# One chip core, attention and a Mish layer: another table for the order of the instructions, with 22 summed sets in place of 17

## The chip, the core and the metric

The kernel runs on one core of a Trainium2 chip. The metric is the device time of one execution in microseconds. The kernel before the change has a median of 687.55 us over 3 runs (686.66 to 688.27).

## The reference

An attention branch and a dense branch with Mish share one input and are mixed by a gate per row (S = 2048 rows, D = 640 columns, 32 heads of 20 columns, F = 1536):

```python
q, k, v = split((x @ wqkv), heads=32)            # Dh = 20
p = softmax(q @ k^T * Dh ** -0.5)
a = (p @ v).reshape(B, S, D) @ wo
h = x @ w1 + b1
b = (h * tanh(softplus(h))) @ w2                 # Mish
g = sigmoid((x * gate_w).sum(-1, keepdims=True))
out = g * a + (1 - g) * b
```

## The kernel before

**Tiles.** Work goes by groups: a group G is four heads (p, 8 of them) by 512 query rows (qc, 4 of them), 32 groups in all. A group's scores are 16 key tiles j by four heads, that is 64 units of 128 keys by 512 queries, each one a matmul on 32 rows of TensorE (L1120) into one of seven banks of PSUM. The eighth bank, `acc`, takes the products of the exponentials with V (L1155), four matmuls of a key tile side by side on the columns of the array.

**Two ways to an exponential.** 1380 of the 2048 units go to ScalarE, one to three banks in one instruction (L1138, the ring `E`). The other 668 go to VectorE: L618 writes an integer whose bits are a rough power of two (tile `T`), and GpSimd corrects it by adding a constant to the bits (L648, `int64_add` on four units at once, 128x2048 two-byte numbers). A set is four such units. A plain set is multiplied three times: as VectorE left it, and after two additions, each time with another scaled copy of V (`VD`, made from `VA` by VectorE at L600). A summed set has one addition, then VectorE sums the two versions (L672, 128x2048), then a second addition; it is multiplied twice. So a summed set costs one sum on VectorE, and saves four matmuls of 512 columns.

**The end of a group.** When a group's last product is in `acc`, VectorE transposes it (L1184), takes reciprocals of the sums (L1191, 128x16), and multiplies (L1198, 128x320, both operands in SBUF). Four transfers on SP's queue then store it to `o_dram`.

**The rest.** The projections, the dense layers and the output projection are "chains" of short matmuls, put between the score matmuls; VectorE takes each chain's result out of PSUM (L787 for q and k, L883 for the first dense layer, L925 for the second, L999 for the output, L841 for V). `Mish` is two long instructions on ScalarE (L904) with a table load on either side. Nearly all transfers stand on SP's queue in one order: loads of k and q tiles (L807, L815), stores (L790, L1231, L932), weights (L476), the second branch's rows (`bl`, L966).

**What sets the order.** A table of steps, `ORDER`, written out as text and read from left to right. Each engine gets its instructions in that order, and waits only for the data and buffers it needs:

```python
steps = {"q": load_q, "k": load_k, "b": load_b, "v": make_vd,
         "d": d_take, "D": d_unit, "S": emit_s, "x": emit_exp,
         "m": lambda: mish(act_q.popleft()), "V": emit_pv,
         "C": begin, "F": run_piece, "f": run_part, "y": vector,
         "p": lambda k, tag: waiting["G"].pop(k)[0](tag)}
for op, a in re.findall(r"([a-zA-Z])([-\d,]*)", ORDER):
    steps[op](*(int(v) for v in a.split(",") if v))
```

`S2,4` computes two score units into banks 4 and 5, `x2` exponentiates the next two on ScalarE, `D0,15,3,6` computes a unit for VectorE into bank 6, `y27` issues VectorE's 27th waiting operation, `p3,7` GpSimd's third addition into tile T7 (a negative number: in place), `V7,-1` the product of key tile 7 from `E`, `F` the next piece of a chain, `f` a quarter of a piece on 32 rows. A third number 1 in `d0,6,1` makes the set a summed one.

Of the kernel before, what the change touches and what calls it, by code (L numbers as in the profile page):

```python
# [19 lines left out]
S2,1 S1,0 S1,6 S1,5 S1,3 C0,4 F x2 C1,1 F0 F0 C3,2 x1 C4,0 F0 F0 y1 x1 F1 F C2,6 x1 x1 y3 F3 y4 F S1,1 S1,0  # L20
C6,3 S1,5 F F y6 v0,0 C5,6 y5 x1 F6 F6 F6 F6 F6 F6 F6 F6 x1 C7,0 y2 F6 F6 F6 x1 F6 F6 F5 F6 S2,1 S1,4 F5 F6 x2
F6 F6 F6 y9 y10 F5 y11 F5 y12 F5 F S2,1 S1,5 y13 y14 S1,3 x1 F C8,4 F7 F7 F7 x2 F V1,-1 x1 V0,-1 F F S2,1 x1
S2,5 F F x2 y15 C9,3 V3,-1 F F F8 F F8 x2 S3,0 F x3 F F8 S2,5 V2,-1 F8 F8 F8 F8 F8 y16 F8 F8 C10,3 F8 d0,6,1
x2 F8 F8 F8 F8 S2,0 F y17 y18 y19 C11,5 x2 F10 y20 F10 S1,2 S1,6 y21 x1 l3 S1,4 F F F10 V5,-1 F10 d0,8,0 F F
S2,1 x1 V4,-1 x1 q1 F F F F y22 F F F D0,15,3,6 S2,3 y23 V6,-1 F F x2 S1,0 S1,2 C12,1 F F11 F11 F11 F11 F11 x2
F11 F11 y24 y25 x1 S1,6 D0,15,2,3 x1 y26 x1 S1,4 F F y27 y28 y29 S1,2 D0,15,0,5 S1,0 x1 F C13,3 F12 y30 F x1 F
S1,6 S1,4 D0,14,3,2 d1,0,0 x1 S1,5 F F F x1 y31 x2 C14,0 F F y32 F D0,15,1,6 S1,1 y33 S1,2 F y34 V7,-1 F F F F
S2,3 D0,14,0,5 F F F F y35 x2 F F S1,6 S1,1 D0,14,1,2 d1,2,0 V9,-1 F V8,-1 F x2 F F F p1,3 F S1,3 y36 S2,4 x1
C15,2 F y38 F y39 V10,-1 y40 F F y41 y42 F d3,4,0 F x1 D0,14,2,6 S2,0 F F y37 y43 p3,7 F x3 V11,-1 p4,1 F S1,5
x2 y44 S1,4 y8 V15,0 y45 V14,0 x1 x1 V12,-1 S1,3 C16,4 D1,15,1,6 x1 D1,15,0,5 S1,2 y7 S2,0 y46 F F F F F p2,-1  # L30
F F x1 S1,3 D1,15,2,6 S1,2 y47 d2,3,0 F x1 V14,1 x1 F F C17,5 V15,1 y48 x1 y49 S2,0 f17,1 y50 D1,14,0,6 x1
V14,2 F D1,15,3,2 S1,3 y51 x2 S1,4 f17,2 F V13,-1 f17,0 D1,14,1,6 S1,0 q2 y52 S1,1 F x2 F p5,7 y53 x2 f17,3
D1,14,2,4 y54 y56 d1,6,0 S2,2 V0,-1 V1,-1 y57 D1,13,0,6 S2,0 p6,5 C18,5 F F d1,1,0 x2 y55 S2,2 y58 S1,4 x2 F F
F V15,0 D1,13,1,6 S1,0 y60 y61 S1,1 V15,1 V15,2 x3 D1,12,0,5 S3,2 V2,-1 x2 l8 C19,6 y62 F F F F F F F
D1,14,3,5 S2,0 V4,-1 F x3 F F y63 x2 y64 p7,8 p8,5 S3,2 V5,-1 x1 y65 V3,-1 C21,2 V14,0 D1,13,3,6 S1,0 e0 S1,1
x2 y66 D2,15,0,5 F l7 y67 F F F D1,13,2,6 S2,3 l0 V14,2 F x2 S1,0 y68 y69 D1,12,3,5 S1,1 d2,7,0 x2 y70 l2
V6,-1 x2 V13,0 D1,12,2,6 S1,2 p9,5 S2,3 d2,0,0 V14,1 x1 V7,-1 y72 V13,1 D1,12,1,5 l6 p10,8 S1,0 C20,2 S1,1 y73
V8,-1 p11,2 F F F F F F x2 p12,5 S3,3 D2,15,3,6 V12,0 y59 F F x2 V13,2 y74 F F x3 y75 S1,0 D2,15,1,6 S1,1
V12,1 V9,-1 y76 S1,3 C22,2 D2,14,0,5 S1,4 F x2 y77 x2 F F F F S2,0 D2,15,2,6 q3 F x2 l5 F F F F S1,4 y78 y79
p13,6 D2,14,3,3 v1,0 S1,5 V10,-1 C23,6 y80 V12,2 x2 y81 F D2,14,1,2 S2,0 x2 V11,-1 F F F y82 S2,3 D2,13,0,5 F  # L40
p14,8 y85 x2 F F S2,1 y86 D2,14,2,0 F F F y87 y89 V0,-1 S1,3 y90 S1,4 y91 D2,13,3,5 p15,5 V15,2 x2 V15,0 S2,0
D2,13,1,2 V15,1 y92 x2 V14,0 V1,-1 y93 d2,3,1 S1,3 x2 D2,12,0,5 S1,4 C24,2 V14,1 F e2 S2,0 x2 D2,13,2,6 y94 x2
F F D2,12,3,3 y95 y96 S2,4 d2,5,0 F F S1,0 D2,12,1,6 S1,1 y97 d3,1,0 V3,-1 x2 x2 p16,8 V14,2 V2,-1 S1,2 C25,5
y98 D2,11,0,4 y88 S1,3 V13,0 x2 F S1,0 D2,12,2,6 p17,6 S1,1 p18,2 y99 F F y101 S1,2 x2 S1,3 D2,11,3,4 F F
p19,0 S1,0 D2,11,1,6 y102 S1,1 d3,7,0 V13,1 x2 V5,-1 x2 l1 V4,-1 y103 S1,2 D3,15,0,4 y105 C26,5 S1,3 y106 F F
S1,0 x2 S1,1 D2,11,2,6 V13,2 F x2 y104 D3,15,3,4 p20,-1 S2,2 F F V12,0 S2,0 y107 V7,-1 V6,-1 x2 p21,2 S1,2
y109 D3,14,0,6 y108 S1,3 D3,14,3,5 V11,0 V12,1 D3,15,1,4 y110 y111 C27,5 x2 x2 S2,0 V11,1 V8,-1 S2,2 D3,13,0,6
y112 F F d3,2,0 y100 y113 x2 x2 F F F D3,15,2,4 S2,0 F y114 F F F D3,13,3,6 S1,2 q4 y115 S1,3 V9,-1 p22,8 x2 F
V11,2 C29,6 S2,0 D3,14,1,4 x2 V10,-1 y116 y117 y118 d3,5,0 F S1,2 k1 D3,12,0,5 S1,3 F F x2 p23,0 p24,3 x2 F
S2,0 x2 D3,14,2,4 y119 V15,0 F y120 y121 D3,12,3,5 S2,2 V15,1 V0,-1 S2,0 D3,13,1,4 y123 x2 y124 V14,0 y125  # L50
V15,2 p25,6 D3,11,0,6 d3,3,0 y126 p26,-1 S2,2 V14,1 V1,-1 C28,6 x2 D3,12,1,4 S2,0 D3,13,2,5 V2,-1 F F V14,2 F
F F x2 F y128 S2,2 x2 D3,11,3,5 S2,0 y127 x2 y129 F F F F V13,0 V3,-1 y130 S2,2 y131 y83 D3,10,0,5 S1,4 C30,6
F F y132 F x2 y84 x1 F F S1,5 y133 p27,6 S1,1 D3,10,3,0 x2 y134 x1 S1,2 V4,-1 V13,1 S1,3 D3,12,2,6 y135 C34,5
# [1392 lines left out]
```

## Time and profile before

| | |
|---|---|
| median of 3 runs | 687.55 us |
| profiled execution | 687.91 us |
| its span, first to last instruction | 686.1 us |
| granted TensorE clock | 0.999 |
| POOL (GpSimd) busy | 358.2 us, 52% of the span |
| idle time before the L648 additions | 313.4 us |
| DMA engines' busy share over the span, queue q1 | 27.1% |

In the rows of the profile each group of instructions is told by line, engine, operation, what it writes and reads, shapes and count; behind the bar stands the idle time of the engine before such instructions and who ended it. In the timeline a row gives the start in us, the length in us, and in brackets the idle time ahead of it. Neighbours of one kind are merged into one row with a count. ScalarE's first exponential starts at 9.05 us; the output's last steps on TensorE begin after 677 us.

### The profile page before, as it was taken

How to read it: one execution, taken by the hardware profiler on the slowest of the kernel's cores; microseconds unless marked ns; L12 is line 12 of the kernel's file. 1: busy time of each engine (PE TensorE's matmuls, PEld its weight loads, DVE VectorE, ACT ScalarE, POOL GpSimd, SP SyncE). 2: the span in 40 equal slices, each digit the busy share in tenths (PEclk: the TensorE clock that was granted, in tenths of full speed). 3: DMA queues.
4: the chain of work that ended last, by engine and by line, in shares of the span. 5: the costliest groups of instructions: out<-in, count | busy, mean ns of one | idle time of the engine just before them, and what ended most of it. 6: DMA issues, size and time to landing. Idle time of an engine off the chain costs nothing. (4 is left out here: it accounts for less than half of the span.)

```text
span 686.1 us, 24551 instructions
## 1 busy us (share of the span) xinstructions
PE 674.1 (98%) x10335; PEld 236.1 (34%) x10335; DVE 607.6 (89%) x1038; ACT 668.4 (97%) x705; POOL 358.2 (52%) x349
## 2 busy tenths in 40 slices
PE   8999999999999999999999999999999999999997
PEld 4433233323323343333333223222243333333333
DVE  5689999998989989999889988999998988899895
ACT  6999999999999999999999999999999999999995
POOL 5045545545454536575645544456646564565542
PEclk9999999999999999999999999999999999999999
DMA  8524331313312122121122213322321213142321
GB/s 169 119 85 79 71 76 47 72 38 79 76 31 52 41 34 39 17 48 29 53 90 48 34 52 73 66 60 34 57 64 62 22 24 67 29 69 57 51 84 59
DMA packets 128542, 40.47 MB, mean 59 GB/s; under 512 B 94960, under 2 KB 127872, under 8 KB 128432
## 3 DMA queue, kind: packets, MB, share of 16 engines
q1 hardware_dynamic: 126032, 38.29, 27.1%
q8 instruction: 81, 1.33, 0.9%
q10 hardware_dynamic: 2400, 0.62, 0.4%
q14 instruction: 29, 0.24, 0.2%
HBM read 22.29 MB, written 12.78 MB: 51 GB/s over the span
## 5 line engine op out<-in xcount | busy, mean ns | idle before, releaser
L1138 ACT ACTIVATE E<-Sp 128x1024 bf16<-128x1024 f32 (+2 forms) x687 | 636.5, 1088 | 6.1 <-PE Sp L1120 5.6
L648 POOL INT64_ADD T<-T x334 | 348.3, 1053 | 313.4 <-DVE T L618 187.8
L618 DVE TENSOR_SCALAR T<-Sp 128x512 int16<-128x512 f32 x668 | 437.8, 682 | 44.6 <-PE Sp L1120 37.3
L1120 PE MATMUL Sp<-qT,kT 32*128 32x512 bf16 x2048 | 262.7, 383 | 4.8 <-DVE T L618 2.1
L1120 PEld LDWEIGHTS <-kT 32*128 32x128 bf16 x2048 | 70.5, 91 | 237.5 <-issue 232.0
L1155 PE MATMUL Sp<-E,VA 128*21 128x512 bf16 x1380 | 128.8, 382 | 0.1
L1155 PE MATMUL Sp<-T,VD 128*21 128x512 bf16 x1268 | 117.2, 382 | 0.0
L702 PE MATMUL Sp<-w_sb,big 128*32 128x320 bf16 x1488 | 75.6, 301 | 0.0
L702 PE MATMUL Sp<-xT,w1t 128*32 128x512 bf16 x940 | 74.2, 382 | 0.0
L1155 PEld LDWEIGHTS <-VA 128*21 128x21 bf16 x2048 | 45.0, 90 | 62.8 <-issue 54.4
L1155 PE MATMUL Sp<-T,VA 128*21 128x512 bf16 x668 | 63.8, 382 | 0.0
L702 PE MATMUL Sp<-xT,ws 128*32 128x512 bf16 x716 | 55.5, 382 | 0.4 <-issue 0.3
L702 PEld LDWEIGHTS <-big 128*32 128x32 bf16 x1488 | 33.3, 95 | 28.3 <-issue 20.1
L1155 PEld LDWEIGHTS <-VD 128*21 128x21 bf16 x1268 | 29.8, 90 | 37.5 <-issue 31.8
L883 DVE TENSOR_SCALAR big<-Sp,b1f 128x512 bf16<-128x512 f32 x48 | 35.7, 743 | 3.0 <-PE Sp L702 2.2
L702 PE MATMUL Sp<-wv,xT 128*32 128x81 bf16 (+2 forms) x960 | 35.0, 256 | 0.0
L702 PE MATMUL Sp<-wo_sb,od 128*32 128x320 bf16 (+1 forms) x604 | 28.9, 300 | 0.6 <-DVE ot L999 0.6
L702 PEld LDWEIGHTS <-w1t 128*32 128x32 bf16 x940 | 20.5, 94 | 25.4 <-issue 18.8
L787 DVE CAST st<-Sp 128x512 bf16<-128x512 f32 x36 | 24.4, 683 | 4.6 <-PE Sp L702 4.4
L702 PEld LDWEIGHTS <-xT 128*32 128x32 bf16 x960 | 21.0, 96 | 11.5 <-issue 6.0
L1184 DVE STREAM_TRANSPOSE T<-Sp 128x512 f32<-128x512 f32 x32 | 22.7, 709 | 2.2 <-PE Sp L1155 1.9
L702 PEld LDWEIGHTS <-ws 128*32 128x32 bf16 x716 | 16.4, 95 | 19.3 <-issue 13.4
(84 smaller groups left out, 242.8 us busy)
## 6 DMA issues: line engine op xcount, KB each, us to landing
w1t<-in_B_w_dram SPq DMA_DIRECT2D x24, 320.0 KB
q_dram<-st SPq DMA_DIRECT2D x20, 128.0 KB
b_dram<-bt SPq DMA_DIRECT2D x16, 160.0 KB
bl<-b_dram SPq DMA_DIRECT2D x16, 160.0 KB
qT<-q_dram SPq DMA_DIRECT2D x124, 20.0 KB
o_dram<-T SPq DMA_DIRECT2D x120, 20.0 KB
out_dram<-ot SPq DMA_DIRECT2D x15, 160.0 KB
kT<-k_dram SPq DMA_DIRECT2D x28, 80.0 KB
```

What stands on the lines that cost most here:

```text
L618: nc.vector.tensor_scalar(out=dst.bitcast(I16), in0=src, scalar1=inv_sqrt_dh * LOG2E * 128.0, scalar2=127.0 * 128.0 + (BETA2 if two else B ...
L648: nc.gpsimd.int64_add(dst[:, :].bitcast(I64), src[:, :].bitcast(I64), n * 0x0001000100010001)
L702: nc.tensor.matmul(out_[k : k + 32], lhsT=lhsT[:, k : k + 32], rhs=rhs, tile_position=(0, k), start=start, stop=ch.done(), skip_group_chec ...
L787: nc.vector.tensor_copy(out=res["st"][:, :], in_=ps[:, :])
L883: nc.vector.tensor_scalar(out=big[:, pair_of(c, ft), (ft % 2) * QC : (ft % 2 + 1) * QC], in0=ps[:, :], scalar1=b1f[:, ft : ft + 1], scalar ...
L1120: nc.tensor.matmul(ps_cols, lhsT=kT[p][32 * t_ : 32 * t_ + 32, j * P : (j + 1) * P], rhs=qT[G][32 * t_ : 32 * t_ + 32, :], tile_position=( ...
L1138: nc.scalar.activation(E[:, x : x + n, :], allb[:, k0 : k0 + n, :], ACT.Exp, scale=inv_sqrt_dh,)
L1155: nc.tensor.matmul(acc[32 * t_ : 32 * t_ + DH + 1, :], lhsT=lhsT, rhs=rhs, start=(pv_done[G] == 0), stop=(pv_done[G] == pv_total[G] - 1), ...
L1184: nc.vector.transpose(out=st["T1"][:, :, :].rearrange("p b r -> p (b r)"), in_=acc[:, :])
```

## The change

Nothing but the table `ORDER` is replaced; every function stays as it is. The new text has one line more, so each line number of the kernel is one higher afterwards (L1138 becomes L1139). Its first and last steps:

```diff
 ORDER = """
-S2,1 S1,0 S1,6 S1,5 S1,3 C0,4 F x2 C1,1 F0 F0 C3,2 x1 C4,0 F0 F0 y1 x1 F1 F C2,6 x1 x1 y3 F3 y4 F S1,1 S1,0
+S1,1 S3,4 x1 C0,3 S1,0 S1,2 x2 F F x1 x1 C1,1 C2,6 F0 C3,4 F0 F0 C4,5 x1 F1 F F3 F2 y3 S1,0 C6,2 y4 S1,1 F F F
...
+V11,0 V9,-1 C183,1 V8,-1 F181 y1007 V11,1 V12,2 V10,-1 V11,2 C182,5 F F y1008 F183 F183 b15 y1009 F183 F183 F
+y1010 F y1013 y1011 y1012
 """
```

Counted over the two tables:

| | before | after |
|---|---|---|
| ScalarE exponentials of 1, 2, 3 banks | 57, 567, 63 (687) | 44, 572, 64 (680) |
| summed sets among the 167 | 17 | 22 |
| products of a key tile with V (four matmuls each) | 829 | 824 |
| GpSimd additions | 334 | 334 |
| VectorE operations that the table issues | 1008 | 1013 |
| quarter pieces `f` of chains on 32 rows | 76 | 68 |
| visits of TensorE to matmuls on 32 rows | 640 | 643 |

**VectorE at the fourth group's end (about 133 us).** `VD` is the scaled copy of V, `T_0_88` the group's output, `rec` the reciprocals. Before:

```order
L787 CAST st<-Sp 128x512
L618 TENSOR_SCALAR T<-Sp 128x512 x2
L1191 RECIPROCAL rec<-T_2708 128x16
L618 TENSOR_SCALAR T<-Sp 128x512
L600 TENSOR_SCALAR VD<-VA 128x7x84 x2
L618 TENSOR_SCALAR T<-Sp 128x512 x2
```

Now:

```order
L788 CAST st<-Sp 128x512
L619 TENSOR_SCALAR T<-Sp 128x512 x3
L601 TENSOR_SCALAR VD<-VA 128x7x84
L1192 RECIPROCAL rec<-T_2672 128x16
L601 TENSOR_SCALAR VD<-VA 128x7x84
L619 TENSOR_SCALAR T<-Sp 128x512
```

The first copy now stands directly behind the L619 that completes a set for GpSimd, and the second behind the reciprocal.

**VectorE near the end of the program (about 642 us).** Before:

```order
L618 TENSOR_SCALAR T<-Sp 128x512 x3
L1191 RECIPROCAL rec<-T_12798 128x16
L1198 TENSOR_TENSOR T_1_89<-T_12798,rec 128x16x20
L618 TENSOR_SCALAR T<-Sp 128x512
L999 SCALAR_TENSOR_TENSOR ot<-Sp,g_t,bl 128x320
```

Now:

```order
L1192 RECIPROCAL rec<-T_12781 128x16
L619 TENSOR_SCALAR T<-Sp 128x512 x3
L1000 SCALAR_TENSOR_TENSOR ot<-Sp,g_t,bl 128x320
L619 TENSOR_SCALAR T<-Sp 128x512
L1199 TENSOR_TENSOR T_1_89<-T_12781,rec 128x16x20
```

The multiplication stood directly behind the reciprocal, two places behind the L618 that completes a set; five instructions now stand between the two, and the L619 that completes a set is four places ahead.

**SP's queue in the last 35 us.** `bl` are rows of the second branch, `od` the transposed attention output. Before:

```order
L932 DMA b_dram<-bt 128x640
L953 DMA_TRANSPOSE od<-o_dram 128x512
L1008 DMA out_dram<-ot 128x640
L966 DMA bl<-b_dram 128x640
L1008 DMA out_dram<-ot 128x640
L966 DMA bl<-b_dram 128x640 x4
```

Now:

```order
L967 DMA bl<-b_dram 128x640
L954 DMA_TRANSPOSE od<-o_dram 128x512
L1009 DMA out_dram<-ot 128x640
L967 DMA bl<-b_dram 128x640
L1009 DMA out_dram<-ot 128x640
L967 DMA bl<-b_dram 128x640 x2
```

One load of `bl` goes ahead of the last transposing load of `od`, and the bunch of four becomes two, with the last one behind one more store of the output.

More of the change, by code (lines that the diff above doesn't have):

```diff
@@ L25 @@
[L25 to L29, printed above, removed]
@@ new lines @@
+p170,1 D17,14,2,6 S1,2 x2 S1,3 f104,3 x2 F p171,4 y548 F F d17,3,0 y549 S1,0 d17,2,0 S1,1 y550 C105,6
+D17,13,0,4 V10,-1 F x2 D17,14,3,5 S1,2 p172,5 S1,3 y551 V11,2 F F x2 v6,0 S2,0 D17,13,1,4 F F q18 S1,2 y552
+y553 y556 S1,3 y557 D17,13,2,5 p173,8 V0,-1 v5,0 x2 V15,1 D17,12,0,4 x2 S2,0 V14,0 p174,4 V15,0 y559 y562 S2,2
+x2 x2 D17,13,3,6 V1,-1 d17,0,0 V14,2 y563 D17,11,0,4 D17,12,1,5 y560 S2,0 V2,-1 x2 V14,1 V15,2 y564 S2,2
+p175,7 D17,12,2,6 V3,-1 y565 V13,0 D17,11,1,5 S1,0 y566 y567 S1,1 V13,1 V4,-1 x2 C106,5 S1,2 D17,12,3,6 x2
@@ new lines @@
+y648 S1,2 D20,12,1,4 y649 p205,4 S1,3 x2 y650 V13,1 V13,0 V14,2 y651 D20,11,3,1 y652 S1,5 x2 S1,6 q22 x2
+d21,7,0 D20,11,0,0 V3,-1 S2,3 p206,5 y653 D20,12,2,2 d20,3,0 V2,-1 C121,1 F F x2 D20,10,0,0 S2,5 y654 V4,-1 x2
+F S2,2 D20,11,1,4 F x2 F y655 S1,5 D20,10,3,0 S1,6 p207,6 y656 x2 H y657 p208,8 V13,2 D20,11,2,4 S2,2 V12,1
+d21,6,0 y658 y659 V12,2 D21,15,0,6 S1,0 x2 S1,1 D21,15,3,5 V12,0 V6,-1 y660 d21,0,0 V11,0 C122,6 S2,3
+D20,10,1,2 F V5,-1 x2 x2 v7,0 S1,0 f122,3 p209,-1 S1,1 y661 D21,14,0,5 F y662 p210,4 F S2,2 f122,1 y664
@@ new lines @@
+d21,5,1 D20,10,2,4 y665 x2 F x2 V11,2 S1,0 D21,14,3,5 S1,1 y666 f122,0 V11,1 V7,-1 D21,15,1,2 y667 S1,3 C123,5
+x2 f122,2 S1,4 y669 V9,-1 V10,0 x2 F S2,0 D21,13,0,6 p211,2 x2 y668 f123,3 p212,-1 V8,-1 S1,2 f123,1
+D21,15,2,4 S1,3 y670 V10,1 V10,2 F d22,4,0 S1,0 x2 y671 S1,1 D21,13,3,6 f123,0 F y663 S1,2 f123,2 S1,3
+D21,14,1,4 F y672 x2 x2 y673 d22,8,0 V0,-1 y675 S1,0 D21,12,0,6 p213,2 S1,1 V15,0 V1,-1 S1,2 D21,14,2,5 S1,3
+y677 C124,6 p214,-1 y674 V15,1 x2 F F x2 D21,12,3,4 d21,1,0 y678 S2,0 F y679 S1,2 D21,13,1,5 p215,3 S1,3 x2
```

581 lines of the change are left out of this document (285 added, 296 removed).

## The prediction

> **What bounds the kernel now.** I read the busy times first, then the waits, then stretches of the span.
>
> ```profile
> span 686.1 us, 24551 instructions
> PE 674.1 (98%) x10335; PEld 236.1 (34%) x10335; DVE 607.6 (89%) x1038; ACT 668.4 (97%) x705; POOL 358.2 (52%) x349
> DVE T L618 <- PE Sp L1120: 37.3, 105, 1.3
> ACT E L1138 <- PE Sp L1120: 5.6, 14, 1.2
> 130.00:150.00 20.00, 19.16 (x267) 5.62 (x268) 19.11 (x31) 19.20 (x20) 9.27 (x9) 1.00 0.27 61
> 150.00:430.00 280.00, 278.99 (x4167) 92.37 (x4159) 252.59 (x415) 279.46 (x287) 150.22 (x143) 1.00 0.23 50
> 430.00:450.00 20.00, 19.42 (x255) 5.15 (x247) 19.27 (x32) 19.54 (x22) 10.51 (x10) 1.00 0.27 42
> ```
>
> The columns of the stretches are: length, busy us of PE, PEld, DVE, ACT and POOL, clock, DMA share, GB/s. ScalarE (ACT) and TensorE (PE) are both full: from 150 to 430 us ScalarE works 279.46 of 280 us. The order can win only what ScalarE loses, and the fourth row says that it waits 14 times for scores from L1120, 5.6 us in all (the third is VectorE's own wait for them). In two short stretches it loses 0.80 us (130 to 150) and 0.46 us (430 to 450), and just there VectorE is as full as the others: 19.11 and 19.27 of 20 us. So the question is which late VectorE work holds up the scores.
>
> **Where the waits come from.** The price list by form, with a stretch of 14 undisturbed exponentials (291 to 303 us) as its second row:
>
> ```profile
> L1138 ACT ACTIVATE E<-Sp 128x1024 bf16<-128x1024 f32 x567 | 537.8, 1084 | 4.6 <-PE Sp L1120 4.2
> L1138 ACT ACTIVATE E<-Sp 128x1024 bf16<-128x1024 f32 x14 | 13.0, 1115 | 0.0
> L1138 ACT ACTIVATE E<-Sp 128x1536 bf16<-128x1536 f32 x63 | 95.7, 1519 | 0.5 <-PE Sp L1120 0.5
> L1138 ACT ACTIVATE E<-Sp 128x512 bf16<-128x512 f32 x57 | 33.0, 649 | 1.0 <-PE Sp L1120 0.9
> L672 DVE TENSOR_TENSOR T<-T 128x2048 bf16<-128x2048 bf16 x17 | 21.4, 1258 | 0.1
> L1198 DVE TENSOR_TENSOR T<-T,rec 128x320 bf16<-128x320 f32 x31 | 18.5, 597 | 0.2
> L600 DVE TENSOR_SCALAR VD<-VA 128x588 bf16<-128x588 bf16 x16 | 9.2, 578 | 0.0
> ```
>
> Now four places in order of time, each from VectorE's late instruction to ScalarE's idle time in brackets; the row at 428.63 is the same multiplication with nothing beside it.
>
> ```profile
> 92.49 1.04 POOL L648 INT64_ADD T<-T  x1 [3.61 <-DVE rec L1191]
> 92.51 1.36 DVE L1198 TENSOR_TENSOR T<-T,rec 128x320 bf16<-128x320 f32 x1
> 94.53 0.37 PE L1120 MATMUL Sp<-qT,kT 32*128 32x512 bf16 x1 [0.47 <-DVE T L618]
> 95.59 2.49 ACT L1138 ACTIVATE E<-Sp 128x512 bf16<-128x512 f32 x4 [0.45 <-PE Sp L1120]
> ...
> 133.39 3.12 POOL L648 INT64_ADD T<-T  x3 [1.48 <-PE Sp L1155]
> 133.56 2.10 DVE L600 TENSOR_SCALAR VD<-VA 128x588 bf16<-128x588 bf16 x2
> 136.30 0.37 PE L1120 MATMUL Sp<-qT,kT 32*128 32x512 bf16 x1 [0.82 <-DVE T L618]
> 137.70 2.05 ACT L1138 ACTIVATE E<-Sp 128x1024 bf16<-128x1024 f32 x2 [0.79 <-PE Sp L1120]
> ...
> 428.63 0.48 DVE L1198 TENSOR_TENSOR T<-T,rec 128x320 bf16<-128x320 f32 x1
> ...
> 437.87 1.28 DVE L1198 TENSOR_TENSOR T<-T,rec 128x320 bf16<-128x320 f32 x1
> 440.32 1.02 ACT L1138 ACTIVATE E<-Sp 128x1024 bf16<-128x1024 f32 x1 [0.27 <-PE Sp L1120]
> 441.53 1.94 ACT L1138 ACTIVATE E<-Sp 128x1024 bf16<-128x1024 f32 x2 [0.19 <-PE Sp L1120]
> ...
> 641.94 1.36 DVE L1198 TENSOR_TENSOR T<-T,rec 128x320 bf16<-128x320 f32 x1
> 644.46 2.51 ACT L1138 ACTIVATE E<-Sp 128x1024 bf16<-128x1024 f32 x3 [0.18 <-PE Sp L1120]
> ```
>
> The chain is the same each time. A GpSimd addition runs (92.49, 1.04 us); a multiplication that needs 0.48 us starts 0.02 us later and ends at 93.87, after the addition's end at 93.53. Everything behind it on VectorE is 0.88 us late, L618 frees a bank late, TensorE's next score waits 0.47 us, and ScalarE 0.45 us. I call this a meeting. ScalarE's idle time at the four places is 0.45 + 0.79 + 0.27 + 0.19 + 0.18 = 1.88 us. An exponential after an idle time also lasts 1.08 us in place of a step of about 0.91 us ((13.0 - 1.115) / 13): five times 0.17 is 0.85. Together 2.73 us. Two transfers cost ScalarE time too:
>
> ```profile
> 426.16 0.39 PE L1120 MATMUL Sp<-qT,kT 32*128 32x512 bf16 x4 [0.61 <-DMA kT<-k_dram]
> 426.69 3.28 ACT L1138 ACTIVATE E<-Sp 128x1536 bf16<-128x1536 f32 x3 [0.46 <-PE Sp L1120]
> ...
> 665.75 6.91 SPq L966 DMA_DIRECT2D bl<-b_dram  x4
> 668.13 0.55 DVE L999 SCALAR_TENSOR_TENSOR ot<-Sp,g_t,bl 128x320 bf16<-128x320 f32 x1 [1.00 <-PE Sp L1155]
> 668.74 0.73 PE L702 MATMUL Sp<-wo_sb,od 128*32 128x320 bf16 x16 [0.62 <-DVE ot L999]
> 669.92 6.66 ACT L1138 ACTIVATE E<-Sp 128x1024 bf16<-128x1024 f32 x6 [0.56 <-PE Sp L1120]
> ```
>
> L999 at 668.13 reads `bl`. L1155, named as its releaser, writes another bank, so I take the load issued from 665.75 on as what it waited for: an inference.
>
> **The change part by part.** First, exponentials: 13 fewer of one bank, 5 more of two, 1 more of three, the same 1380 banks in 7 fewer instructions. Durations grow 0.435 us a bank (649, 1084, 1519 ns), so of a step of 0.911 us only 0.04 belongs to the instruction: 7 x 0.04 = -0.3 us. If nothing overlapped it would be 1.084 - 0.870 = 0.21 each, -1.5; if it is hidden, 0. I take -0.3, since exponentials run back to back nearly everywhere. (The Trainium skill, "ScalarE: Activation LUTs", section "What ACT_TABLE_LOAD costs", gives 186 ns fixed and about 93 ns of overlap between neighbours; 7 x 93 ns would be -0.65, an estimate from that page; the row's 0.04 decides.)
>
> Second, TensorE: five products fewer, three more visits to the 32-row matmuls, and two pieces of a chain that were four quarters on those rows become whole. The prices:
>
> ```profile
> 304.60 0.39 PE L1120 MATMUL Sp<-qT,kT 32*128 32x512 bf16 x3
> 304.93 0.40 PE L1155 MATMUL Sp<-E,VA 128*21 128x512 bf16 x4
> 305.15 0.39 PE L1155 MATMUL Sp<-T,VA 128*21 128x512 bf16 x4
> ```
>
> A product takes 0.22 us (304.93 to 305.15), a visit to the 32-row matmuls 0.33 (304.60 to 304.93). Five products save 5 x 0.22 = 1.1; three more visits cost up to 1.0, two whole pieces up to 0.4. Between -1.1 and +0.3; I take 0, because ScalarE, as full as TensorE, keeps its own pace.
>
> Third, five more sums: 5 x 1.258 = 6.3 us on VectorE. Their cover is VectorE's idle time, 686.1 - 607.6 = 78.5 us; without it, all 6.3 us count. The 17 sums of before start no idle time of ScalarE at the places above, so I take +0.5.
>
> Fourth, the meetings. In the order of before, 7 of the 31 multiplications stand directly behind the reciprocal, three of them two places behind the L618 that completes a set: these are the ones at 92, 437 and 641 us. In the new order 5 stand so, and two of them (the 1st and the 26th) two places behind a completed set; none is at the old places. At 133 us one copy of `VD` goes ahead of the addition and one can still meet it. So -2.73 for the old places, if they all go (0 if none does). For new meetings: two multiplications as above, the second copy, two more multiplications with one instruction between, and two sums side by side where GpSimd is due, six in all. An unhidden one costs 2.73 / 5 = 0.55. I count a third of them, as VectorE has 11% to spare over the span: 6 x 0.55 / 3 = +1.1 (0 to 3.3).
>
> Fifth, transfers. Of the `bl` loads one now goes ahead of the last transposing load, and the bunch of four is broken up: -0.56 - 0.17 = -0.73 (0 if L999 waited for something else). The k tile at 426 us stands behind the same weight load as before, only the second tile's four loads no longer follow it: half of 0.46 + 0.17, -0.3 (0 to -0.63).
>
> Sum: -0.3 + 0 + 0.5 - 2.73 + 1.1 - 0.73 - 0.3 = -2.46. The profiled execution took 687.91 us, 1.8 more than its span, and becomes 685.45; the median of the runs lies 0.36 below it, so 685.1. What is late next: scores in the stretches where both engines are full, with no VectorE cause, which the order cannot give back.
>
> **The rivals.** (1) The meetings only move: all six new ones reach ScalarE, 3.3 in place of 1.1. Then -0.26, 687.3, no change. For it: the number of additions is the same, and the chances to meet grew by five sums. Against: the four costly places have all been taken apart.
>
> (2) Slower: VectorE becomes the engine that frees banks late, because of the sums. With all of 6.3 us on the path the sum is -2.96 + 6.3 = +3.3, 690.9; it turns to the slower side once 4.4 us of the 6.3 show, and 690.0 is the middle of that. For it: in the stretches at 130 and 430 us VectorE has 0.9 and 0.7 us of 20 spare, less than one sum, and a sum holds GpSimd up as well:
>
> ```profile
> 234.18 1.21 DVE L672 TENSOR_TENSOR T<-T 128x2048 bf16<-128x2048 bf16 x1
> 234.36 1.93 POOL L648 INT64_ADD T<-T  x1 [2.26 <-DVE T L618]
> ```
>
> The addition that starts during the sum lasts 1.93 us in place of 1.04, so its set is complete later and its products wait. Against: over the span VectorE has 11% to spare. (The Trainium skill, "SBUF — State Buffer", section "SBUF: two separate sides", has one lock for the pair of ports that VectorE and GpSimd share, held for a whole instruction by whoever starts first. The rows at 92 and 234 us agree; by the rule the five added sums would be 5 x 1.258 = 6.3 us more in which no addition gets on, an estimate.)
>
> (3) Deeper: no new meeting and no sum costs anything, and both transfers go: -0.3 - 2.73 - 0.73 - 0.63 = -4.4, 683.2. For it: most of VectorE's work has cover. Against: six new chances to meet.
>
> **How the numbers follow.** A measurement of this kernel can tell 0.2%, that is 1.4 us, from no change. The forecast near 685.1 has 0.43, own range 683.9 to 686.2; deeper 0.12; no change 0.24; slower 0.21. Faster is 0.43 + 0.12 = 0.55. Below, the range reaches past the deeper case by 0.8, for the unlikely -1.5 of the exponentials in part: 682.4. Above, it reaches nearly to the middle of the slower case: 689.8.
>
> **What would show it.** ScalarE's idle time before L1139 falls from 6.1 us (its wait for scores from 5.6) to about 4; the L1199 mean falls from 597 ns towards 540, L601 from 578 towards 400; no PE wait above 0.4 us for the L619 bank near 95, 136 and 440 us; no wait for `ot` near 669 us. The step on sums is wrong if VectorE's wait for scores (37.3 us at L618 before) falls by the full 6 us while ScalarE idles more. The forecast is wrong if L1199 and L601 are quicker and the time is not: then the scores were late for TensorE's own sake.

## The result and the profile after

The changed kernel has a median of 685.86 us (684.88 to 686.69, 8 runs) against 687.37 us for the kernel before on the same chip: ratio 0.9974, 95% interval 0.9963 to 0.9985. A second series gave 685.16 against 686.93 us: 0.9973 (0.9963 to 0.9984). So the change takes off some 1.5 to 1.8 us, about 0.26%, 0.7 to 1.0 us less than the sum of the prediction. One execution of the run e9_sums_small below, at a granted clock of 0.863, took 716.0 us and is left out of its median.

The profiled execution took 685.10 us. The first rows are from its page, the next three from its table of waits (waiting engine, tile, line, releaser; us in total, times, longest), the last three from its groups by form.

```profile
span 683.2 us, 24486 instructions
PE 673.0 (99%) x10315; PEld 236.4 (35%) x10315; DVE 606.5 (89%) x1043; ACT 667.3 (98%) x698; POOL 359.1 (53%) x349
...
L1139 ACT ACTIVATE E<-Sp 128x1024 bf16<-128x1024 f32 (+2 forms) x680 | 635.3, 1090 | 4.3 <-PE Sp L1121 3.9
```

```profile
DVE T L619 <- PE Sp L1121: 37.8, 101, 1.3
...
ACT E L1139 <- PE Sp L1121: 3.9, 9, 1.2
...
PE Sp L1156 <- POOL T L649: 1.4, 3, 0.6
```

```profile
L673 DVE TENSOR_TENSOR T<-T 128x2048 bf16<-128x2048 bf16 x22 | 26.7, 1219 | 0.0
...
L1199 DVE TENSOR_TENSOR T<-T,rec 128x320 bf16<-128x320 f32 x31 | 17.2, 555 | 0.2
L601 DVE TENSOR_SCALAR VD<-VA 128x588 bf16<-128x588 bf16 x16 | 5.2, 324 | 0.0
```

ScalarE waits for scores 3.9 us in place of 5.6. The copies of `VD` fell from 578 to 324 ns, the multiplications at a group's end only from 597 to 555. The third row of the waits is new in the list: three times TensorE waits for a tile of GpSimd's, 1.4 us in all; the kernel before has no such wait.

The two short stretches that were not full before are full now (length; busy us of PE, PEld, DVE, ACT, POOL):

```profile
130.00:150.00 20.00, 20.00 (x278) 5.88 (x278) 18.92 (x33) 20.00 (x21) 9.88 (x10) 1.00 0.23 52
...
430.00:450.00 20.00, 19.99 (x265) 5.68 (x261) 18.79 (x32) 20.00 (x23) 10.93 (x11) 1.00 0.34 77
```

Both tables exponentiate the same 1380 banks, so ScalarE's progress can be compared bank by bank. This table is worked out from the two traces: the start of the exponential that takes up the given number of banks done, and how far the new order is ahead. An exponential after an idle time takes some 0.17 us more than the step between undisturbed ones, so a difference can be complete a bank or two later.

```
banks done   before      after     after is ahead by
   58         37.90      37.37       0.53
   99         56.76      56.57       0.18
  181         95.59      95.05       0.54
  190         99.97      99.14       0.83
  270        137.70     135.95       1.75
  511        261.48     260.34       1.13
  851        417.51     416.07       1.44
  870        426.69     424.69       2.00
  901        441.53     438.93       2.61
  984        479.85     476.97       2.89
 1213        597.84     595.52       2.31
 1271        624.51     622.50       2.01
 1280        628.65     627.17       1.47
 1314        644.46     642.51       1.94
 1366        669.92     667.08       2.84
```

It gains at the old meetings (95 to 100, 137, 440, 480, 644 us) and at the `bl` wait (670). It loses some 0.55 us at 57 (it is 0.72 ahead at 94 banks done and 0.18 at 99), and about 0.55 to 0.8 us each near 261, 597 and 628 us. Much of the gain near 427 us belongs to this one execution of the kernel before: the runs below that keep its table are ahead by as much there.

The 0.53 us at 38 us hides two things. The three runs below that keep the table of before up to there are 0.5 to 0.7 us ahead of this execution already at 36.5 us, where the changed kernel is only 0.1 ahead; so the steps of its start cost it 0.4 to 0.5 us, by a cause that stays open. Right behind, at 37 to 40 us, it gains 0.6 us, because a meeting that the prediction had not listed is gone. In the kernel before, both copies of `VD` run beside additions:

```profile
35.48 1.09 DVE L600 TENSOR_SCALAR VD<-VA 128x588 bf16<-128x588 bf16 x1
...
36.80 0.81 DVE L600 TENSOR_SCALAR VD<-VA 128x588 bf16<-128x588 bf16 x1
...
37.40 1.57 ACT L1138 ACTIVATE E<-Sp 128x512 bf16<-128x512 f32 x3 [0.27 <-PE Sp L1120]
```

In the changed kernel they last 0.33 and 0.32 us (33.27 and 34.11 us), and ScalarE has no idle time there.

One of the three losing places, from the timeline of the changed kernel; the first fence is GpSimd alone in a narrow window, the second all engines:

```profile
591.77 1.93 POOL L649 INT64_ADD T<-T  x1 [1.47 <-DVE T L619]
```

```profile
591.59 1.22 DVE L673 TENSOR_TENSOR T<-T 128x2048 bf16<-128x2048 bf16 x1
...
594.77 0.40 PE L1156 MATMUL Sp<-T,VD 128*21 128x512 bf16 x4 [0.59 <-POOL T L649]
595.10 0.40 PE L1121 MATMUL Sp<-qT,kT 32*128 32x512 bf16 x4
...
595.52 0.60 ACT L1139 ACTIVATE E<-Sp 128x512 bf16<-128x512 f32 x1 [0.44 <-PE Sp L1121]
```

A sum starts at 591.59, an addition 0.18 us later. The addition lasts 1.93 us in place of 1.04, and the next one in GpSimd's queue is 0.89 us late. The product that reads the tile of that next one stands ahead of the next scores on TensorE and waits 0.59 us, so the scores are late and ScalarE idles 0.44 us. This is the meeting of the prediction with the roles exchanged: GpSimd is held up, and TensorE waits for it.

### The profile page after: what moved, and what is told of

Same layout as the page of the kernel before. It is cut to its first block, busy times and chain, and to the rows that moved or that the text cites. A ratio compares the mean times of both kernels' runs of the same rounds, so it can differ in the third digit from the quotient of the medians.

```text
span 683.2 us, 24486 instructions
## 1 busy us (share of the span) xinstructions
PE 673.0 (99%) x10315; PEld 236.4 (35%) x10315; DVE 606.5 (89%) x1043; ACT 667.3 (98%) x698; POOL 359.1 (53%) x349
## 5 line engine op out<-in xcount | busy, mean ns | idle before, releaser
L1139 ACT ACTIVATE E<-Sp 128x1024 bf16<-128x1024 f32 (+2 forms) x680 | 635.3, 1090 | 4.3 <-PE Sp L1121 3.9
L619 DVE TENSOR_SCALAR T<-Sp 128x512 int16<-128x512 f32 x668 | 437.8, 683 | 47.1 <-PE Sp L1121 37.8
L1156 PE MATMUL Sp<-T,VD 128*21 128x512 bf16 x1248 | 114.7, 382 | 1.4 <-POOL T L649 1.4
L703 PE MATMUL Sp<-wv,xT 128*32 128x81 bf16 (+2 forms) x960 | 37.5, 257 | 0.1
L884 DVE TENSOR_SCALAR big<-Sp,b1f 128x512 bf16<-128x512 f32 x48 | 35.7, 744 | 2.0 <-PE Sp L703 0.7
L673 DVE TENSOR_TENSOR T<-T 128x2048 bf16<-128x2048 bf16 x22 | 26.7, 1219 | 0.0
```

Source lines behind the costliest of these rows:

```text
L619: nc.vector.tensor_scalar(out=dst.bitcast(I16), in0=src, scalar1=inv_sqrt_dh * LOG2E * 128.0, scalar2=127.0 * 128.0 + (BETA2 if two else B ...
L673: nc.vector.tensor_tensor(out=d[0][:, :], in0=d[0][:, :], in1=d["T"][:, :], op=ALU.add)
L703: nc.tensor.matmul(out_[k : k + 32], lhsT=lhsT[:, k : k + 32], rhs=rhs, tile_position=(0, k), start=start, stop=ch.done(), skip_group_chec ...
L884: nc.vector.tensor_scalar(out=big[:, pair_of(c, ft), (ft % 2) * QC : (ft % 2 + 1) * QC], in0=ps[:, :], scalar1=b1f[:, ft : ft + 1], scalar ...
L1139: nc.scalar.activation(E[:, x : x + n, :], allb[:, k0 : k0 + n, :], ACT.Exp, scale=inv_sqrt_dh,)
L1156: nc.tensor.matmul(acc[32 * t_ : 32 * t_ + DH + 1, :], lhsT=lhsT, rhs=rhs, start=(pv_done[G] == 0), stop=(pv_done[G] == pv_total[G] - 1), ...
```

## The experiments

Every run was compared with the kernel before on its own chip. In the diffs only the steps around an edit are shown of each long line. The first two undo two causes in the table of before, one at a time, and the third both.

**Meetings alone.**

```diff
-q5 y136 l4 V13,2 S2,3 y137
+q5 l4 V13,2 S2,3 y137
...
-x2 y138 S1,5
+x2 y138 y136 S1,5
...
-D6,14,0,5 y142 y143 S1,2
+D6,14,0,5 S1,2
...
-S2,0 y202 V13,2
+S2,0 y202 y142 y143 V13,2
```

y646, y707 and y953 move in the same way, behind y649, y708 and y955.

> The table of before, with only five VectorE places changed: four multiplications L1198 (those at 92, 437, 476 and 641 us) and the pair of VD copies L600 (133 us) are issued a few VectorE instructions later, so that none starts right beside a GpSimd addition. Theory (meetings cost ScalarE time and TensorE can use it): the idle times 0.45 + 0.79 + 0.27 + 0.19 + 0.18 us go, with up to 5 x 0.17 us of slower first exponentials: 1.9 to 2.7 us less than before, ratio 0.9960 to 0.9973; mean of L1198 from 597 to about 510 ns, of L600 from 578 to about 390 ns. Rival (TensorE and ScalarE are both full, so a stall that is taken away comes back within a few us): VectorE's instructions get as short, but the time stays within 0.5 us of before, ratio 0.9993 to 1.0007, and ScalarE's idle time before L1138 stays near 6.1 us.

Measured: 684.39 us (684.01 to 684.65) against 687.04, ratio 0.9960 (0.9947 to 0.9972), 2.65 us less. By form:

```profile
L1138 ACT ACTIVATE E<-Sp 128x1024 bf16<-128x1024 f32 x567 | 537.8, 1087 | 2.9 <-PE Sp L1120 2.7
...
L1198 DVE TENSOR_TENSOR T<-T,rec 128x320 bf16<-128x320 f32 x31 | 15.9, 512 | 0.1
L600 DVE TENSOR_SCALAR VD<-VA 128x588 bf16<-128x588 bf16 x16 | 7.6, 483 | 0.0
```

The idle time went and did not come back, so the rival falls. The mean of `VD` fell only to 483 ns, not to 390: the moved pair lasts 0.33 and 0.32 us, but four other copies that this edit leaves, at 35, 36, 244 and 407 us, still last 0.81 to 1.09. Behind the two at 35 and 36 us ScalarE still idles 0.27 us, as in the kernel before. With the transfers untouched, this run has no wait near 426 us, but it has the one for `bl`:

```profile
664.05 0.55 DVE L999 SCALAR_TENSOR_TENSOR ot<-Sp,g_t,bl 128x320 bf16<-128x320 f32 x1 [0.93 <-DMA bl<-b_dram]
...
664.66 0.73 PE L702 MATMUL Sp<-wo_sb,od 128*32 128x320 bf16 x16 [0.54 <-DVE ot L999]
...
665.84 3.06 ACT L1138 ACTIVATE E<-Sp 128x1024 bf16<-128x1024 f32 x3 [0.49 <-PE Sp L1120]
```

Here the profile itself names the load as L999's releaser, which the prediction had inferred.

**Transfers alone.**

```diff
-S1,0 k6 S1,1 F F S1,3 y622
+S1,0 S1,1 F F S1,3 y622
...
-S1,0 y629 S1,1
+S1,0 y629 k6 S1,1
...
-V2,-1 y983 D31,13,1,0
+V2,-1 y983 b11 D31,13,1,0
...
-C176,0 b11 F x2
+C176,0 F x2
```

> The table of before, with only two transfers moved: one bl load goes ahead of where it stood (from 665.75 us to about 662 us), and the four loads of the second k tile go about 5 us later. Theory (both waits were the transfers' own): PE's wait for ot near 668.7 us (0.62) and ScalarE's idle 0.56 us behind it go, 0.7 us; at 426 us up to 0.6 us: together 0.7 to 1.3 us less, ratio 0.9981 to 0.9990. Rival (L999 waited for something else, and the k tile is late because of the weight load ahead of it): no change at both places, ratio 0.9995 to 1.0005, and the waits at 426 and 668 us stay.

Measured: 686.43 us (686.03 to 687.50) against 687.04, ratio 0.9991 (0.9982 to 0.9999), 0.6 us less. L999 no longer waits for a load, and ScalarE runs through:

```profile
665.70 3.39 ACT L1138 ACTIVATE E<-Sp 128x1024 bf16<-128x1024 f32 x4
...
666.11 0.55 DVE L999 SCALAR_TENSOR_TENSOR ot<-Sp,g_t,bl 128x320 bf16<-128x320 f32 x1 [0.17 <-PE Sp L702]
```

The wait at 426 us is absent too, but it was absent in the run ahead of it as well, which left both transfers in place. SP's queue before that time, in the kernel before, and then with the meetings moved:

```profile
419.32 1.58 SPq L476 DMA_DIRECT2D w1t<-in_B_w_dram  x1
420.95 4.34 SPq L807 DMA_DIRECT2D kT<-k_dram  x8
```

```profile
417.17 0.42 SPq L476 DMA_DIRECT2D w1t<-in_B_w_dram  x1
417.63 5.44 SPq L807 DMA_DIRECT2D kT<-k_dram  x8
```

In this run the weight load takes 1.54 us and only four loads follow it. The wait was there only where the weight load held the queue for 1.58 us and all eight loads followed it. How often that happens is not settled; the 0.6 us of this run, just under the expected 0.7 to 1.3, are no more than the `bl` wait alone is worth.

**Both.** The edits of the two runs together.

> The table of before with the edits of the two runs ahead of it together (five VectorE places and two transfers). Theory (independent stalls add up): 2.6 to 4.0 us less than before, ratio 0.9942 to 0.9962, so more than the whole change brought (1.5 us). Rival (the stalls hide one another, or the engines take them back): no more than the better of the two alone, at most 1.5 us, ratio 0.9978 or above.

Measured: 683.68 us (683.37 to 684.16), ratio 0.9951 (0.9937 to 0.9964), 3.36 us less; 2.65 + 0.61 is 3.26. The two add up, and together they bring about twice what the whole change did. So the change gave something back.

**The products that wait.** In the table of after, three steps `V` go later on TensorE, nothing else:

```diff
-V13,1 V14,0 V14,1 y383 x2 S1,0 y385 x2 S1,1 D11,12,2,6 C78,5 F x2 F V1,-1
+V13,1 V14,0 y383 x2 S1,0 y385 x2 S1,1 D11,12,2,6 C78,5 F x2 F V14,1 V1,-1
...
-V9,-1 V12,1 S1,2 C156,6 S1,3 D28,13,0,5 S1,4 F y889 F F F d28,7,0 F V10,-1
+V9,-1 S1,2 C156,6 S1,3 D28,13,0,5 S1,4 F y889 F F F d28,7,0 F V12,1 V10,-1
...
-V13,2 F x2 S1,3 D29,10,2,5 y939 S1,4 V3,-1
+F x2 S1,3 D29,10,2,5 y939 S1,4 V13,2 V3,-1
```

> The table of after, with three products of a set moved 7 to 13 steps later on TensorE. They are those at 259.52, 594.77 and 626.16 us, which wait 0.40, 0.59 and 0.39 us for a GpSimd addition that was held up behind a sum (L673). Theory (this is where the change gave time back): ScalarE's idle 0.51 + 0.44 + 0.47 us goes, 1.4 us, with 3 x 0.17 us up to 1.9 us less than after: 684.0 to 684.5 us, ratio to before 0.9946 to 0.9954. Rival (the late addition holds VectorE or the tile ring up in the same way, so the wait moves to another buffer): the time of after, 685.9 us, ratio 0.9970 to 0.9978.

Measured: 683.65 us (683.37 to 684.20), ratio 0.9950 (0.9938 to 0.9963). Bank by bank against the changed kernel, this execution gains 0.66 us at 260, 0.49 at 595 and 0.58 at 627 us, and nothing elsewhere: 1.7 us. The place shown above in this run:

```profile
591.89 5.37 ACT L1139 ACTIVATE E<-Sp 128x1536 bf16<-128x1536 f32 x6
...
593.48 0.40 PE L1121 MATMUL Sp<-qT,kT 32*128 32x512 bf16 x4
...
594.56 0.40 PE L1156 MATMUL Sp<-T,VD 128*21 128x512 bf16 x4
```

The scores now go ahead of the product, which waits for nothing, and ScalarE has no idle time.

**The new meetings.** On top of these three edits, four multiplications go clear of the additions beside them:

```diff
-S1,5 y73 p10,2
+S1,5 p10,2
...
-F y77 F F F
+F y77 y73 F F F
```

y140, y164 and y276 move behind y143, y183 and y281.

> The table of after with the three late products (as in the run e4_late_products) and four multiplications L1199 (54.1, 96.2, 121.7 and 187.4 us) a few VectorE instructions later, clear of the additions beside them. Theory (each new meeting costs only where ScalarE was seen to idle behind it: 0.25 us at 56.6, 0.17 at 123.9, each with 0.17 us of a slower first exponential): 0.4 to 0.9 us less than with the late products alone (683.65 us): 682.8 to 683.3, ratio to before 0.9937 to 0.9945. Rival (all four are covered by other work, the idle there has another cause): as with the late products alone, 683.5 to 683.8, ratio 0.995.

Measured: 683.47 us (683.26 to 685.25), ratio 0.9953 (0.9941 to 0.9964): no gain that can be told from the run with late products. L1199 fell from 555 to 488 ns. ScalarE's idle time at 56.6 us is gone, the one at 123.8 is not, though the multiplication at 121.7 was the nearest late work:

```profile
121.64 2.03 ACT L1139 ACTIVATE E<-Sp 128x1024 bf16<-128x1024 f32 x2
123.83 3.98 ACT L1139 ACTIVATE E<-Sp 128x1024 bf16<-128x1024 f32 x4 [0.17 <-PE Sp L1121]
```

Bank by bank against the run with late products, this run gains 0.48 us at 57 and loses 0.18, 0.21 and 0.15 us near 101, 126 and 194 us, behind the three places to which the other multiplications went. At 126 us, for example, L1199 and the L884 behind it now stand ahead of four L619, which start at 124.49 in place of 124.33 us, and ScalarE idles a new 0.10 us. So one of the four meetings had a price, and the other three moves cost about as much as that one brought. That those three were covered where they stood is read from the traces: behind them the changed kernel has no idle time of ScalarE but the 0.17 us at 124 us, and the kernel before has the same one (124.87 us). The expectation of 0.4 to 0.9 us was too high, and it had put that idle time down to the wrong neighbour.

**What a sum costs.** Four runs. In the first, each sum is preceded by an instruction of the same size that changes nothing:

```diff
         def total():
+            nc.vector.tensor_tensor(out=d[0][:, :], in0=d[0][:, :], in1=d[0][:, :], op=ALU.max)
             nc.vector.tensor_tensor(out=d[0][:, :], in0=d[0][:, :], in1=d["T"][:, :], op=ALU.add)
```

> The table of after, but ahead of each of the 22 sums VectorE takes the maximum of the one operand with itself, 128x2048, which changes nothing in the result: 22 more instructions of about 1.2 us, 26.5 us more of VectorE in all. The prediction's step (most of a sum is covered, 0.1 us of each shows): +2 us, 688 us, ratio to before 1.000. First rival (VectorE frees the banks late, so a sum counts in full): +20 to +27 us, 706 to 713, ratio 1.027 to 1.037. Second rival (a sum costs through the addition that it holds up: the three places where that already happens grow by 1.2 us each, and some more places begin): +4 to +8 us, 690 to 694, ratio 1.004 to 1.010.

Measured: 715.12 us (712.35 to 718.81), ratio 1.0409 (1.0386 to 1.0432). Against the changed kernel's 0.9973 that is 30 us for 22 instructions; the first rival's 27 is the nearest. TensorE's wait for banks that L619 frees grows from 0.4 to 9.2 us, and new is a wait of 7.4 us for the sums themselves; so with this much more work VectorE does free the banks late. The granted clock lay between 0.988 and 0.998 in these executions (712.35 us at 0.998, 718.81 at 0.988), so some 3 of the 30 us may be the clock's. Is a sum that dear, then? The opposite edit says no:

```diff
-            nc.vector.tensor_tensor(out=d[0][:, :], in0=d[0][:, :], in1=d["T"][:, :], op=ALU.add)
+            nc.vector.tensor_tensor(out=d[0][:, 0:16], in0=d[0][:, 0:16], in1=d["T"][:, 0:16], op=ALU.add)
```

> The table of after; each of the 22 sums adds only the first 16 of its 2048 columns, so nearly all of the summing is left out (the products and additions stay). VectorE loses about 22 x 1.1 = 24 us of work, and no addition is held up by a sum. The prediction's step (0.1 us of a sum shows) with the three held additions found since (1.4 to 1.9 us): 3.6 to 4.1 us less than after, about 681.5, ratio to before 0.991 to 0.9925. First rival (a sum counts in full, as the doubled sums did at 1.3 us each): 24 to 29 us less, 656 to 661, ratio 0.957 to 0.963. Second rival (sums are covered altogether and the held additions have another cause): 0 to 1 us less, ratio 0.996 to 0.998.

Measured: 683.42 us (683.29 to 683.87, four executions), ratio 0.9948 (0.9934 to 0.9962). VectorE has 23.3 us less to do in the 22 sums (26.7 to 3.4), and the time falls by 1.7 us (0.9973 to 0.9948). Bank by bank the gain is 0.7 us at 260, 0.6 to 0.8 from 595 to 597 and 0.4 at 627, the same three places as with the late products. That is the 1.4 to 1.9 us of the held additions alone; the further 0.1 us for each sum does not show, and the first rival, a sum that counts in full, falls for the sums that are there. The rows at the middle one:

```profile
590.96 0.16 DVE L673 TENSOR_TENSOR T<-T 128x16 bf16<-128x16 bf16 x1
591.14 2.05 POOL L649 INT64_ADD T<-T  x2 [1.47 <-DVE T L673]
...
593.24 0.40 PE L1156 MATMUL Sp<-T,VD 128*21 128x512 bf16 x4
```

Two additions take 2.05 us, none is held up, and the product comes without a wait. The third run puts only a 128x512 instruction ahead of each sum:

```diff
+            nc.vector.tensor_tensor(out=d[0][:, 0:QC], in0=d[0][:, 0:QC], in1=d[0][:, 0:QC], op=ALU.max)
```

> The table of after; ahead of each of the 22 sums VectorE takes the maximum of a 128x512 part with itself, which changes nothing in the result: about 0.3 us more each, 22 x 0.3 = 6.8 us in all. If VectorE's delay counts from the first tenth of a microsecond on, as 1.3 us for 1.2 at the doubled sums could be read: +6 to +8 us, 692 to 694, ratio to before 1.006 to 1.009. If there is cover for about one sum at each place, which the sum itself does not use up: 0 to +1.5 us, 685.5 to 687, ratio 0.997 to 0.9995. Between the two, +2 to +5, would say that some places have cover and some have none.

Measured: 693.74 us (693.29 to 694.33), ratio 1.0098 (1.0082 to 1.0113), 8.6 us above the changed kernel by the two ratios, a little more than the first expectation; the second, cover for about one more sum at each place, falls. The groups by form, and then the timeline of the place known from above (the added line makes each later line number one higher):

```profile
L674 DVE TENSOR_TENSOR T<-T 128x2048 bf16<-128x2048 bf16 x22 | 29.8, 1355 | 0.8
...
L673 DVE TENSOR_TENSOR T<-T 128x512 bf16<-128x512 bf16 x22 | 9.2, 420 | 0.1
```

```profile
599.16 0.42 DVE L673 TENSOR_TENSOR T<-T 128x512 bf16<-128x512 bf16 x1
599.34 1.13 POOL L649 INT64_ADD T<-T  x1 [1.47 <-DVE T L619]
...
599.61 1.94 DVE L674 TENSOR_TENSOR T<-T 128x2048 bf16<-128x2048 bf16 x1
...
601.60 0.40 PE L1157 MATMUL Sp<-T,VA 128*21 128x512 bf16 x4 [0.85 <-DVE T L674]
...
602.74 1.02 ACT L1140 ACTIVATE E<-Sp 128x1024 bf16<-128x1024 f32 x1 [1.01 <-PE Sp L1122]
```

The instruction lasts 0.42 us, not the 0.3 that I had expected. At this place it also turns round who starts first: the addition gets in between, and now the sum lasts 1.94 us in place of 1.22. VectorE has 9.2 + 3.1 = 12.3 us more to do, and the time grows by some 8.6. ScalarE's wait for scores shows that the price comes from many places, more of them the longer the delay: 3.9 us in 9 waits in the changed kernel, 7.3 in 15 here, 23.4 in 30 with the sums twice.

The fourth run joins the small sums and the late products:

> The table of after with both edits that each brought about 1.8 us: the sums add only 16 of their 2048 columns (most of the summing is left out), and the three late products stand later. Theory (sums cost only through the three held additions, so the two edits remove the same idle time): no less than either alone, 683.3 to 683.8 us, ratio to before 0.9945 to 0.9953. Rival (two separate causes): both gains, 3.5 us less than after, about 681.8 us, ratio 0.9922 to 0.9930.

Measured: 683.31 us (683.17 to 684.39), ratio 0.9949 (0.9937 to 0.9962), the same as either alone. The changed kernel itself once more, beside it on the same chip:

> The changed kernel itself once more, beside the run e11_small_late on the same chip. Theory (the late products and the small sums remove what the change gave back): 685.0 to 685.9 us, ratio to before 0.9970 to 0.9980, so 1.5 to 2.0 us above e11_small_late. Rival (the gains of those runs were the chip's): equal to e11_small_late within 0.5 us. The profile should show the idle times of about 0.5 us near 260, 595 and 627 us again.

Measured: 685.16 us (685.04 to 685.38), ratio 0.9973 (0.9963 to 0.9984), with idle times of 0.52, 0.45 and 0.47 us at 260.43, 595.64 and 627.28 us. So the 22 sums cost 1.8 us in all, through the additions that they hold up at three places; the bank-by-bank comparison shows nothing beyond that.

**Are these the five added sums?** Only one of them is. Followed step by step through the two tables, the sum at 591.59 us (group 27, key tile 12) is one of the five that the kernel before lacks. The sums at 256.35 us (group 11, key tile 14) and 623.88 us (group 29, key tile 12) stand in both. The first of these holds up the same addition in the kernel before, where it costs nothing. Both kernels, before and then after; the rows of GpSimd are from narrow windows:

```profile
258.30 1.20 DVE L672 TENSOR_TENSOR T<-T 128x2048 bf16<-128x2048 bf16 x1
258.47 1.93 POOL L648 INT64_ADD T<-T  x1 [1.79 <-DVE T L618]
...
261.63 0.39 PE L1155 MATMUL Sp<-T,VD 128*21 128x512 bf16 x4
```

```profile
256.35 1.20 DVE L673 TENSOR_TENSOR T<-T 128x2048 bf16<-128x2048 bf16 x1
256.52 1.93 POOL L649 INT64_ADD T<-T  x1 [1.60 <-DVE T L619]
...
259.52 0.40 PE L1156 MATMUL Sp<-T,VD 128*21 128x512 bf16 x4 [0.40 <-POOL T L649]
```

In both, the next addition ends 2.95 us after the held one starts. The product that reads its tile starts 3.16 us after that start in the kernel before; now TensorE is ready for it after 2.60 us. The new order has put it 0.56 us nearer. At 627 us the two instructions have changed places. In the kernel before, the addition (625.31 us, 1.04) stands ahead of the sum (625.90, 1.52); now it starts 0.23 us behind the sum:

```profile
623.88 1.33 DVE L673 TENSOR_TENSOR T<-T 128x2048 bf16<-128x2048 bf16 x1
...
626.16 0.40 PE L1156 MATMUL Sp<-T,VD 128*21 128x512 bf16 x4 [0.39 <-POOL T L649]
```

So of the 1.8 us some 0.6 belong to an added sum and 1.2 to the order around two sums that were there already. The kernel before has three additions held up behind a sum (1.86 to 1.93 us, at 234, 258 and 270 us) and no wait of TensorE for them; that its 17 sums cost nothing is read from this, no run tests it.

**The price of an exponential.** In the table of after, 50 steps `x2` in a row (290 to about 342 us) become `x1 x1`.

> The table of after with 50 exponentials of two banks (from 290 to about 350 us) written as two of one bank each: the same banks, 50 instructions more. The prediction's step (0.04 us an instruction, from the step between exponentials): +2.0 us, or +2.5 by two steps of 0.477 against one of 0.903; 687.9 to 688.4, ratio to before 1.0007 to 1.0015. Rival (no overlap between neighbours; 0.21 us an instruction, from the durations): +10.7 us, 696.6, ratio 1.013. In a sentence by itself: by the Trainium skill, ScalarE: Activation LUTs, section What ACT_TABLE_LOAD costs, 93 ns each would be +4.7 us, an estimate from that page.

Measured: 689.16 us (688.46 to 690.58), ratio 1.0031 (1.0019 to 1.0043), 4.0 us more by the ratios, between the step's 2.0 to 2.5 and the rival's 10.7. Bank by bank, ScalarE goes from 0.17 us ahead of the changed kernel at 289 us to 2.67 behind it at 342: 2.8 us for 50 instructions, 0.056 each. Another 0.8 us, of which some 0.3 come back soon after, is lost at one place behind the stretch:

```profile
361.42 0.40 PE L1156 MATMUL Sp<-E,VA 128*21 128x512 bf16 x4 [0.46 <-ACT E L1139]
...
361.92 1.02 ACT L1139 ACTIVATE E<-Sp 128x1024 bf16<-128x1024 f32 x1 [0.55 <-PE Sp L1156]
```

TensorE waits for an exponential that has become late, and ScalarE then for TensorE. The Trainium skill (ScalarE: Activation LUTs, What ACT_TABLE_LOAD costs) gives 186 ns fixed and about 93 ns of overlap between neighbours; 50 times the 93 ns that remain would be 4.7 us, an estimate. The measured 0.056 us each lies below that.

**An idle time that is in both kernels.** On top of the run with the moved multiplications, two score units go ahead of the last 12 of 32 short matmuls near 656 us, behind which ScalarE idles 0.46 us in every kernel so far:

```diff
-F172 F172 F F F S2,4 S2,2 x2
+F172 F172 S2,4 F F F S2,2 x2
```

> The table of the run e5_free_c with one more edit: in the stretch where TensorE runs 32 short matmuls of the output projection in a row (655 to 656.4 us of the run with late products) two score units go ahead of the last 12 of them. Theory (this idle of 0.46 us, which before has too and the change left alone, is TensorE's own order, so it can be had back): 0.3 to 0.6 us less than e5_free_c, minus up to 0.3 for one more visit to the 32-row matmuls: 682.3 to 683.3, ratio 0.0 to 0.0009 below that of e5_free_c. Rival (the banks are not free earlier): no difference, and the idle of 0.46 us stays near 656 us.

Measured: 684.07 us (683.54 to 684.45), ratio 0.9955 (0.9943 to 0.9967), not better. Before this edit and with it, from the two timelines:

```profile
657.10 4.69 ACT L1139 ACTIVATE E<-Sp 128x1024 bf16<-128x1024 f32 x5 [0.46 <-PE Sp L1121]
```

```profile
659.64 2.05 ACT L1139 ACTIVATE E<-Sp 128x1024 bf16<-128x1024 f32 x2 [0.46 <-PE Sp L1121]
```

The idle time moved by two exponentials and kept its length. Here both the theory and the rival fall: the banks were free earlier (two score units run at 656.76 us, ahead of the last 12 short matmuls), and it did not help. That is a case in which a stall only moves. That TensorE simply has that much to do there is my reading of the two timelines; no run tests it.

## Why the prediction was right, and where its terms were off

The forecast's mechanism, removed meetings and transfer waits with a part given back, is what the runs show; how the part was given back is not. The forecast size was -2.46 us; measured are -1.5 and -1.8. Point by point:

- **Old meetings, -2.73.** Right: -2.65 (ratio 0.9947 to 0.9972) when they alone are taken apart, of which 0.27 by the bank-by-bank comparison is at 480 us, a place that the step had not priced. Idle time plus 0.17 us for each first exponential was the right price, and the rival of that run, that such a stall comes back, is refuted for these five places. The change removed one more meeting, at 37 us, worth some 0.6 us, which the step had not seen.
- **`bl`, -0.73.** Right: 0.6 us by itself, 0.7 on top of the moved meetings (684.39 to 683.68 us), and the inferred releaser was confirmed.
- **The k tile, -0.3.** Not borne out. The step read a wait of one profiled execution as a property of the order; the next run had the same eight loads in the same order and no wait.
- **Exponentials, -0.3.** Right: 7 x 0.056 is -0.4.
- **New meetings, +1.1.** Too high. Of the two multiplications named, the 1st came as said (54.06 us, 1.36 us long) and cost 0.5 us; the 26th (560.65 us, 0.49 us long) met no addition. The second copy at 133 us met nothing either, 0.27 us. Three other multiplications were lengthened (0.73, 0.91 and 0.96 us, at 96, 122 and 187 us), and of the two sums side by side one held an addition up (234.02 us, 1.94 us long), all without a price that the traces show. So rival (1), in which all six reach ScalarE, falls. "A third of them" was the guess of the step; one in six would have done.
- **Five more sums, +0.5.** The size is about right, by luck. One of the five costs some 0.6 us, through the mechanism of rival (2), a sum that holds an addition up and so makes its set late, which was not put into the sum. The step's own ground, VectorE's idle time of 78.5 us over the span as cover, was the wrong measure: 23 us less of sums bring 1.7 us, 12 us more cost 8.6.
- **The order around the other sums: no term.** This is the largest thing that the sum lacks. Two sums that both tables have cost some 1.2 us now and nothing before, because the new order put one product nearer to the addition that it needs and turned round a sum and an addition at the other place. The prediction looked for what holds VectorE up and had no term for what TensorE reads from GpSimd.
- **The start: no term.** Some 0.4 us are lost ahead of 37 us; the cause stays open.
- **TensorE, 0.** Not measured by itself. The measured terms, -0.4 + 0.6 + 1.2 - 2.65 - 0.6 + 0.5 + 0.4 - 0.7 = -1.65, lie between the two measured totals and leave some 0.2 us either way for it.

So the errors went opposite ways. The order around the other sums (1.2 us) and the start (0.4) were missing and the k tile's 0.3 did not come; the new meetings were 0.6 too dear, and the meeting at 37 us (0.6) came on top. That the total is off by no more than 0.7 to 1.0 us is in part luck. Of the signs named, those for the meetings and for `ot` came as said (ScalarE's idle 6.1 to 4.3 us, L601 to 324 ns; L1199 to 555 in place of 540). The sign named for the step on sums did not show: VectorE's wait for scores stayed (37.3 to 37.8 us). That sign looked for a VectorE without slack, but what a sum did was done to GpSimd, and its sign was the new wait of TensorE for `T`.

## What to carry to other kernels

An engine's idle time over the span is no cover: look at the few microseconds around each long instruction, and ask which other engine it holds up and who reads that engine's result next. The same sum beside the same addition cost nothing with the reader 0.56 us further off. Where an in-order engine waits for a late result, moving the reader behind the next useful work (three steps here, 1.7 us) can be worth as much as removing the delay. Before a wait in a profile becomes a term, look for it in a second execution.

The run with late products, 683.65 us, is faster than both kernels (ratio to before 0.9950, against 0.9973 and 0.9974 for the changed kernel; the intervals meet at 0.9963); the one with four multiplications moved as well, 683.47, cannot be told from it.

## What the runs showed of the hardware

- Which of two instructions starts first decides who waits, and both cases occur at one place: with the sum ahead, the addition lasted 1.93 us and the sum 1.22 (591 us, after); with 0.42 us put ahead of the sum, the addition lasted 1.13 and the sum 1.94 (599 us). The one that is held up lasts 0.7 to 0.9 us longer.
- Such a turn makes the time jump: 22 small instructions that run for 9.2 us made the 22 sums 3.1 us longer as well.
- An exponential more costs ScalarE 0.056 us where it is busy throughout, though one of one bank is shown with a length of 0.63 us (the mean of 44 in the changed kernel).
